# Tile 0's three attention units respaced, and the last tile's weight conversions and load moved later, in a fused attention and two-layer kernel

## The chip, the cores and the metric

The kernel runs on one core of a Trainium2 chip. The metric is the device time of one execution in microseconds (us). The engines are named as the profile names them: PE (TensorE, matrix products), PEld (its weight loads), DVE (VectorE), ACT (ScalarE), POOL (GpSimd) and SP (SyncE, which here only starts DMA transfers; SPq is its queue). Each engine runs its own instructions strictly in order, and waits on the others by semaphores.

## The reference, cut to what matters

```python
# 1. chunked attention, 4 batches x 8 heads x 768 positions x 64: chunks of 32 queries see
#    16 keys to the left, the chunk, 8 to the right, and 8 memory keys
scores = scale * q_c @ k_full.T;  a = softmax(scores);  out_c = a @ v_full
# 2. first layer on 3072 tokens of 512: F1 = 2048
h = x @ w_in;  g = maximum(h, 0) + log1p(exp(-abs(h)));  x1 = g @ w_out
# 3. second layer: F2 = 1536
y = ((x1 @ w_a) * (x1 @ w_b)) @ w_o2
```

## The kernel before, in words

The 3072 tokens are cut into 8 tiles of 384. Every fp32 product is made of three matmuls on split values: a value is rounded to the fp32r type (its high part) and the remainder is kept (its low part), and high x high, high x low and low x high are added up in PSUM.

**Phase 1** runs over tiles t = 0 to 7 and in each over 16 f-steps of 128 of the 2048 hidden columns. An f-step is `emit_h` (12 matmuls into `ph`), `emit_soft` (ACT: abs, exp, ln into `e`; DVE: `g`; then ACT writes the high part `g..h` and DVE or POOL the low part `g..l`), and two steps later (LAG = 2) `emit_x1` (12 matmuls into the four banks `px`). `ph` has two buffers (tag "h"), so `ph` of step f+2 waits until `g` of step f has been read. After step 15 the four `px` are copied out (`xo`, DVE) and stored to DRAM (`x1_scratch`).

**Phase 2** runs over the same 8 tiles: `load_x1` loads a tile back (`xr`) and splits it (`x[:, 0]` a cast on DVE, `x[:, 1]` a subtraction on POOL); 12 steps make `pab` (24 matmuls), the product `c`, and `py`. Three `yo` copies per tile go to the output.

**Weights.** In tile 0 the weights of phase 1 are fetched and converted between the f-steps: a conversion is ACT `raw`, two DVE operations on `tmp`, an ACT cast into `w` and a DVE subtraction into `w` (lines 102 to 113). In tile 7 the weights of phase 2 are fetched and converted the same way, one conversion in an even f-step and two in an odd one.

**Attention.** Tile 0's attention comes ahead of everything, in `Block`s. The tokens of tile t+1 are made during tile t by three `Unit`s of 128 queries: units 3, 4 and 5 in tile 0, units 6, 7, 8 in tile 1, and so on. A unit's steps are: `turn` (DVE transposes k and q into `kt`, `qt`; ACT adds the memory keys to `kt`), `scores` (32 small matmuls into two `sc` banks), `soft` (DVE masks, ACT eight exps into `sm`), `norm_v` (DVE divides), `flip_p` (8 transposes on PE into two `pa` banks, which ACT copies into `af`), `values` (32 matmuls into `pxa`), and `place` (ACT and DVE write the high and low part into the next tile's `x`). `sc`, `pa` and `pxa` share two PSUM buffers (tag "att"), and `kt`, `qt`, `sm` and `af` have one buffer each.

**What sets the order.** A list `plan` holds each step with a due time in slots, two slots to an f-step: slot 2f stands between `emit_soft` of step f and `emit_x1` of step f-2, and slot 2f+1 behind that `emit_x1`. A step is written out at the first slot that isn't below its time. The first three units take their times from `EARLY_STEPS` (offsets) with `place` at `EARLY_AT + EARLY_BY * i` or later. In tile 0 the order on all engines is the written one; in tiles 1 to 7 that holds for PE and DVE alone, and in phase 2 for PE alone; a scheduler places the rest, and it may move instructions of a later stage ahead (the first `raw` of phase 2 stands on ACT in tile 0).

The lines of the plan:

```python
for i, unit in enumerate(units[UPT:]):
    at = 2 * NF1 * (i + 1) // UPT - START
    if i < EARLY:
        at = max(at, EARLY_AT + EARLY_BY * i)
    steps = EARLY_STEPS if i < EARLY else STEPS
    plan += [(at + d - steps[-1][0], i, getattr(unit, step)) for d, step in steps]
```

Of the kernel before, what the change touches and what calls it, by code (L numbers as in the profile page):

```python
# [9 lines left out]
F32 = mybir.dt.float32  # L10
# [3 lines left out]
ALU = mybir.AluOpType  # L14
# [3 lines left out]
TT = 384  # L18
# [3 lines left out]
         (3, "values"), (3.1, "place"))  # L22
START = 1.7
SETS = 1
EARLY_STEPS = ((-7.5, "turn"), (-5.3, "scores"), (-5.2, "soft"), (-3, "norm_v"), (-1.5, "flip_p"),
               (1, "values"), (2, "place"))
EARLY, EARLY_AT, EARLY_BY = 3, 14.5, 8.25

ROUND = ((2, "normal"), (4, "place"), (0, "turn"), (2, "flip"), (1, "scores"), (3, "values"))
EARLY_RAW = (0, 1, 2, 3, 5, 7)  # L30
# [2 lines left out]
CV_ROUND = 1  # L33
CV_AT = (10, 1.5)
LATE = 4
OUT_TAGS = "eegg"


@with_exitstack
def attn_moe_moe2(ctx: ExitStack, tc: tile.TileContext, q, k, v, mem_k, mem_v,  # L40
                  w_in, w_out, w_a, w_b, w_o2, out):
    nc = tc.nc
# [5 lines left out]
    P = 128  # L48
# [17 lines left out]
        name=nc.get_next_instruction_name(), act_func_set_id=6, ins=[], outs=[]))  # L66
# [6 lines left out]
    late = {}  # L73
# [17 lines left out]
    def convert_a(dst, key):  # L91

        u, raw = dst[key]
        words = raw.rearrange("p (n two) -> p two n", two=2)
        low, high = words[:, 0], words[:, 1]
        top = high.bitcast(F32)
        val = mp.tile([P, 512], U32, tag="tmp", name=f"tmp{u}", bufs=2)

        nc.scalar.activation(top, top, AF.Prelu, scale=2.0 ** -112, alpha=-(2.0 ** 32))  # L102

        nc.vector.tensor_scalar(val, low, 29, None, ALU.logical_shift_right)  # L104
        nc.vector.scalar_tensor_tensor(val, high, 3, val, ALU.logical_shift_left, ALU.bitwise_or)  # L105
        dst[key] = u, val.bitcast(F32)
# [25 lines left out]
    def phase2_key(i):  # L132
        f, which = divmod(i, 3)
        return (wab, (which, f)) if which < 2 else (w2o, f)
# [294 lines left out]
# [6 lines that stand above are left out]
# [14 lines left out]
    def split(val, name, engine=nc.gpsimd, between=None):  # L449
        hi = mp.tile([P, TT], F32R, tag="gh", name=name + "h", bufs=3)  # L450
        lo = mp.tile([P, TT], F32R, tag="gl", name=name + "l", bufs=3)
        nc.scalar.copy(hi, val)
        if between:
            between()
        engine.tensor_tensor(lo, val, hi.bitcast(F32), ALU.subtract)
        return hi, lo
# [12 lines left out]
    def emit_soft(t, f, ph, engine=nc.gpsimd, one=None, two=None):  # L469
        e = mp.tile([P, TT], F32, tag="e", name=f"e{t}_{f}")  # L470
        nc.scalar.activation(e, ph, AF.Abs)  # L471
        nc.scalar.activation(e, e, AF.Exp, scale=-1.0)  # L472
        nc.scalar.activation(e, e, AF.Ln, bias=1.0)  # L473
        g = mp.tile([P, TT], F32, tag="g", name=f"g{t}_{f}")
        nc.vector.scalar_tensor_tensor(g, ph, 0.0, e, ALU.max, ALU.add)  # L475
        if one:
            one()
        gt[t, f] = split(g, f"g{t}_{f}", engine, two)

    def emit_x1(t, f):  # L480
# [9 lines left out]
        if f == NF1 - 1:  # L490
            for i in range(KT):
                o = mp.tile([P, TT], F32, tag=OUT_TAGS[i], name=f"xo{t}_{i}")
                nc.vector.tensor_copy(o, acc[t][i][:, :TT])
# [6 lines left out]
    def load_x1(t):  # L500
        raw = late["x"].tile([P, KT, TT], F32, tag="xr", name=f"xr{t}", bufs=1)
        nc.sync.dma_start(raw, x1d[t])
        x = mp.tile([P, 2, KT, TT], F32R, tag="x", name=f"x1_{t}")
        nc.vector.tensor_copy(x[:, 0], raw)  # L504
        nc.gpsimd.tensor_tensor(x[:, 1], raw, x[:, 0].bitcast(F32), ALU.subtract)  # L505
        x1[t] = x

    ct = {}
# [23 lines left out]
    def emit_y(t, f):  # L532
        chh, chl = ct.pop((t, f))
        w = w2o[f]
        if f == 0:
            acc[t] = [ps.tile([P, 512], F32, tag=f"acc{i}", name=f"py{t}_{i}", bufs=1) for i in range(TT // P)]
        for i in range(TT // P):
            s = slice(i * P, (i + 1) * P)
            for m, (a, c) in enumerate(((chh[:, s], w[:, 0]), (chh[:, s], w[:, 1]), (chl[:, s], w[:, 0]))):
                nc.tensor.matmul(acc[t][i], lhsT=a, rhs=c, start=f == 0 and m == 0, stop=f == NF2 - 1 and m == 2)  # L540
        if f == NF2 - 1:
            for i in range(TT // P):
                o = late["x"].tile([P, 512], F32, tag="o", name=f"yo{t}_{i}", bufs=2)
                (nc.vector.tensor_copy if i % 2 else nc.scalar.copy)(o, acc[t][i])
                nc.sync.dma_start(out[t * TT + i * P:t * TT + (i + 1) * P, :], o)
            del acc[t]


    def order():
# [46 lines left out]
        def convert_2(half):  # L596
            n = n_cv2[half]
            if n < (n2, n_cv2[0])[half]:
                if half == 0:
                    convert_a(*phase2_key(n))  # L600
                else:
                    convert_b(*phase2_key(n), late["w"] if n < LATE else None)
                n_cv2[half] += 1

        for t in range(NTILE):
            if t == 1:
                early.close()
                early.enter_context(tc.manual_schedule(engines={engines["P"], engines["V"]}))
            if t == NTILE - 1:
                assert not plan  # L610
                actx.close()
                late["x"] = ctx.enter_context(tc.tile_pool(name="late", bufs=1))
                late["w"] = ctx.enter_context(tc.tile_pool(name="latew", bufs=LATE))
                load_x1(0)
            for f in range(NF1):
                ph = emit_h(t, f)
                if t == 0:
                    due = min(CV_AT[0] + int(CV_AT[1] * (f + 1)), len(uses))
                    fetch_to(due + AHEAD)
                    more = n_cv[0] + 1 < due  # L620
                    convert_1(0)
                    emit_soft(t, f, ph, nc.vector, partial(convert_1, 1), partial(convert_1, 0) if more else None)
                    if more or due == len(uses):
                        convert_1(1)
                elif t < NTILE - 1:
                    emit_soft(t, f, ph)
                else:
                    while n2 < n2_all and n2 < LATE + 2 * max(0, f - LAG):
                        fetch2(n2)
                        n2 += 1  # L630
                    more = f % 2
                    convert_2(0)
                    emit_soft(t, f, ph, nc.vector, partial(convert_2, 1), partial(convert_2, 0) if more else None)
                    if more:
                        convert_2(1)
                att_at(2 * (NF1 * t + f))
                if len(pend) >= LAG:
                    emit_x1(*pend.pop(0))
                pend.append((t, f))
                att_at(2 * (NF1 * t + f) + 1)  # L640
# [55 lines left out]
```

## Time and profile before

| what | us |
|---|---|
| three executions | 1309.62, 1312.18, 1312.55; median 1312.18 |
| the profiled execution, its own time | 1311.32 |
| its span, first to last instruction | 1309.5 |
| PE busy in the span | 1237.2 (94%) |
| DVE busy | 473.4 (36%) |
| ACT busy | 534.7 (41%) |
| POOL busy | 247.6 (19%) |

The span is what the trace shows; 1.8 us of the execution lie outside it. Tile 0's f-steps stand from about 51 to 161 us, tiles 1 to 6 from there to about 611, tile 7 to about 697, and phase 2 from there to the end. In such a profile an engine's idle time counts only where another engine ends up waiting for it, so the table says which engine is nearest to full, and the waits say where time can be won.

### The profile page before, as it was taken

The page shows a single profiled execution, that of the slowest core. Times are in us where ns is not written, and L with a number is a line of the kernel's source. Part 1 is how long each engine was busy: PE and PEld are TensorE (multiplying, and loading weights), DVE is VectorE, ACT ScalarE, POOL GpSimd, SP SyncE. Part 2 cuts the span into 40 slices and gives each one's busy share as a digit, 9 for nine tenths or more (in the row PEclk, how much of TensorE's full clock was granted, in tenths as well). Part 3 has the DMA queues.
Part 4 walks back from the last instruction along what each step waited for, and adds up shares of the span by engine and source line. Part 5 has one row for each costly group of instructions (what it writes and reads, how often), then busy time and mean ns, then how long its engine had stood idle before and what let it go on. Part 6 is the DMA issues. An engine that isn't in the chain of part 4 may idle for free.

```text
span 1309.5 us, 20027 instructions
## 1 busy us (share of the span) xinstructions
PE 1237.2 (94%) x7872; PEld 1170.1 (89%) x7872; DVE 473.4 (36%) x1283; ACT 534.7 (41%) x1328; POOL 247.6 (19%) x233
## 2 busy tenths in 40 slices
PE   5768799999999999999798999999999999999998
PEld 4667699999999999999798999999999999999997
DVE  4767544544444454544678410111101011011100
ACT  4767556555556556554685211111111111111111
POOL 1000023223222322323001011211212121121111
PEclk9879899999999999999899999999999999999999
DMA  8872412213041312211775000010101001000000
GB/s 175 205 246 60 90 37 46 54 35 72 12 73 37 60 48 36 62 23 41 241 227 175 1 26 25 1 49 1 49 1 41 9 10 40 1 25 1 25 1 25
DMA packets 170169, 77.99 MB, mean 60 GB/s; under 512 B 137691, under 2 KB 162395, under 8 KB 170075
## 3 DMA queue, kind: packets, MB, share of 16 engines
q1 hardware_dynamic: 169563, 76.64, 22.1%
q8 instruction: 62, 1.02, 0.3%
q14 instruction: 32, 0.26, 0.1%
q0 software_dynamic: 512, 0.07, 0.0%
HBM read 64.09 MB, written 12.58 MB: 59 GB/s over the span
## 4 chain that ended last, share of the span: by engine, by line
PE 84%; DVE 5%; SPq 3%; ACT 3%; DMA 3%; issue 1%; DVEq 0%; ACTq 0%
PE pab L520 31%; PE ph L465 18%; PE px L488 17%; PE py L540 15%; DMA raw<-in_moe_w_out_dram 2%; PE sc L372 1%; PE pxa L415 1%; SPq L267 1%; DVE w L113 1%; DVE tmp L105 1%; ACT e L472 1%; SPq L264 1%; ACT e L471 1%; ACT e L473 1%; DVE g L475 0%
## 5 line engine op out<-in xcount | busy, mean ns | idle before, releaser
L520 PE MATMUL pab<-x,w 128*128 128x384 f32 x2304 | 418.8, 336 | 4.1 <-issue 4.1
L520 PEld LDWEIGHTS pab<-x,w 128*128 128x128 f32 x2304 | 405.9, 188 | 12.6 <-issue 4.4
L465 PE MATMUL ph<-x,w 128*128 128x384 f32 x1536 | 298.3, 342 | 13.5 <-ACT x L422 8.2
L465 PEld LDWEIGHTS ph<-x,w 128*128 128x128 f32 x1536 | 272.9, 192 | 20.1 <-ACT x L422 9.4
L529 DVE TENSOR_TENSOR c<-pab,a 128x384 f32<-128x384 f32 x96 | 53.6, 558 | 493.5 <-PE pab L520 493.5
L475 DVE SCALAR_TENSOR_TENSOR g<-ph,e 128x384 f32<-128x384 f32 x128 | 71.2, 557 | 257.0 <-ACT e L473 253.3
L527 ACT COPY a<-pab 128x384 f32<-128x384 f32 x96 | 46.1, 480 | 260.4 <-PE pab L520 260.4
L471 ACT ACTIVATE e<-ph 128x384 f32<-128x384 f32 x128 | 62.3, 486 | 132.2 <-PE ph L465 119.5
L390 DVE STREAM_TRANSPOSE af<-sm 32x256 f32<-32x256 f32 x180 | 78.2, 435 | 2.5
L473 ACT ACTIVATE e<-e 128x384 f32<-128x384 f32 x128 | 67.3, 526 | 3.8
L472 ACT ACTIVATE e<-e 128x384 f32<-128x384 f32 x128 | 67.3, 526 | 3.8
L329 ACT ACTIVATE sm<-sm,st 128x96 f32<-128x96 f32 x168 | 60.5, 362 | 4.7 <-DVE st L325 4.7
L505 POOL TENSOR_TENSOR x<-xr,x 128x1536 fp32r<-128x1536 f32 x8 | 28.4, 3554 | 153.5 <-DVE x L504 148.7
L105 DVE SCALAR_TENSOR_TENSOR tmp<-raw,tmp 128x512 uint32<-128x512 uint32 x68 | 50.2, 739 | 14.4 <-ACT raw L102 11.0
L113 DVE TENSOR_TENSOR w<-tmp,w 128x512 fp32r<-128x512 f32 x68 | 46.9, 689 | 16.9 <-ACT w L112 16.8
L102 ACT ACTIVATE raw<-raw 128x512 f32<-128x512 f32 x68 | 45.4, 673 | 15.4 <-DMA raw<-in_moe_w_in_dram 7.1
L112 ACT CAST w<-tmp 128x512 fp32r<-128x512 f32 x68 | 41.6, 613 | 17.2 <-DVE tmp L105 17.1
L195 POOL DMA_DIRECT2D mem_n<-in_mem_k_dram x16 | 8.9, 560 | 155.8 <-DVE mem_t L353 155.8
L336 POOL TENSOR_TENSOR sm<-sm,st 128x768 f32<-128x768 f32 x18 | 26.5, 1472 | 60.1 <-DVE st L334 46.9
L104 DVE TENSOR_SCALAR tmp<-raw 128x512 uint32<-128x512 uint32 x68 | 31.9, 469 | 5.0 <-DMA raw<-in_moe_w_in_dram 4.6
L325 DVE CUSTOM_DVE_ANT_0 sm<-sc,mask 128x96 f32<-128x96 f32 x168 | 31.4, 253 | 3.8 <-PE sc L372 3.8
L329 ACT ACTIVATION_READ_ACCUMULATOR sm<-sm,st 128x1 f32 x168 | 31.4, 187 | 0.0
(251 smaller groups left out, 1851.7 us busy)
## 6 DMA issues: line engine op xcount, KB each, us to landing
raw<-in_moe_w_out_dram SPq DMA_DIRECT2D x28, 512.0 KB
raw<-in_moe_w_in_dram SPq DMA_DIRECT2D x16, 512.0 KB
vn<-in_v_dram SPq DMA_DIRECT2D x35, 176.0 KB
raw<-in_moe_w_a_dram SPq DMA_DIRECT2D x12, 512.0 KB
x_scratch<-xo SPq DMA_DIRECT2D x32, 192.0 KB
xr<-x_scratch SPq DMA_DIRECT2D x8, 768.0 KB
raw<-in_moe_w_b_dram SPq DMA_DIRECT2D x12, 512.0 KB
out_dram<-yo SPq DMA_DIRECT2D x24, 256.0 KB
```

The costliest lines, as they stand in the source:

```text
L105: nc.vector.scalar_tensor_tensor(val, high, 3, val, ALU.logical_shift_left, ALU.bitwise_or)
L113: nc.vector.tensor_tensor(w[:, 1], val, w[:, 0].bitcast(F32), ALU.subtract)
L329: nc.scalar.activation(sm[:, h], sm[:, h], AF.Exp, bias=st[:, 0, h:h + 1], scale=-1.0, accum_out=st[:, 1, h:h + 1])
L390: nc.vector.transpose(out=af[32 * kb:32 * kb + 32, x], in_=self.sm[32 * x:32 * x + 32, :, 32 * kb:32 * kb + 32])
L465: nc.tensor.matmul(ph, lhsT=a, rhs=c, start=n == 0, stop=n == 3 * KT - 1)
L471: nc.scalar.activation(e, ph, AF.Abs)
L472: nc.scalar.activation(e, e, AF.Exp, scale=-1.0)
L473: nc.scalar.activation(e, e, AF.Ln, bias=1.0)
L475: nc.vector.scalar_tensor_tensor(g, ph, 0.0, e, ALU.max, ALU.add)
L488: nc.tensor.matmul(acc[t][i][:, :TT], lhsT=a, rhs=c, start=f == 0 and m == 0, stop=f == NF1 - 1 and m == 2)
L520: nc.tensor.matmul(p, lhsT=a, rhs=c, start=n == 0, stop=n == 3 * KT - 1)
L540: nc.tensor.matmul(acc[t][i], lhsT=a, rhs=c, start=f == 0 and m == 0, stop=f == NF2 - 1 and m == 2)
```

## The change

It does five things. In tile 0 the three units get other offsets: `turn` 13 slots ahead of `place` instead of 9.5, `scores` 10 instead of 7.3, `norm_v` 7 instead of 5, `flip_p` 4 instead of 3.5; and `place` is due at slots 17.4, 24.2 and 31 instead of 14.5, 22.75 and 31, so that a unit's `turn` and `scores` come ahead of the `values` and `place` of the unit in front. In tile 7 the conversions start at step 2 instead of step 0. The first `load_x1` is written at step 7 of tile 7 instead of ahead of it. Its subtraction goes to DVE instead of POOL (for the first tile alone). And `yo` gets three buffers instead of two.

```diff
-EARLY_STEPS = ((-7.5, "turn"), (-5.3, "scores"), (-5.2, "soft"), (-3, "norm_v"), (-1.5, "flip_p"),
-               (1, "values"), (2, "place"))
-EARLY, EARLY_AT, EARLY_BY = 3, 14.5, 8.25
+EARLY_STEPS = ((-13, "turn"), (-10, "scores"), (-9.9, "soft"), (-7, "norm_v"), (-4, "flip_p"),
+               (-1, "values"), (0, "place"))
+EARLY, EARLY_AT, EARLY_BY = 3, 17.4, 6.8
...
+CV2_AT = 2
+X1_AT = 7
...
-        nc.gpsimd.tensor_tensor(x[:, 1], raw, x[:, 0].bitcast(F32), ALU.subtract)
+        (nc.vector if t == 0 else nc.gpsimd).tensor_tensor(x[:, 1], raw, x[:, 0].bitcast(F32), ALU.subtract)
...
-                o = late["x"].tile([P, 512], F32, tag="o", name=f"yo{t}_{i}", bufs=2)
+                o = late["x"].tile([P, 512], F32, tag="o", name=f"yo{t}_{i}", bufs=TT // P)
...
-                load_x1(0)
...
-                    more = f % 2
-                    convert_2(0)
-                    emit_soft(t, f, ph, nc.vector, partial(convert_2, 1), partial(convert_2, 0) if more else None)
+                    if f == X1_AT:
+                        load_x1(0)
+                    more = f >= CV2_AT and f % 2
+                    if f >= CV2_AT:
+                        convert_2(0)
+                    emit_soft(t, f, ph, nc.vector, partial(convert_2, 1) if f >= CV2_AT else None, partial(convert_2, 0) if more else None)
```

What this does to the order of the instructions is seen in three places. In a name such as `ph0_6_950` the first number is the tile and the second the f-step; in `pa0_3_938` the first is the bank and the second the unit; the last is a buffer's number.

PE in tile 0, at the transposes of unit 3 (`flip_p`); before:

```order
L488 MATMUL px0_3_728<-g0_3h_779,w9_641 128x384
L404 MATMUL pa0_3_938<-ident_75,sm3_852 96x128 x4
L404 MATMUL pa1_3_944<-ident_75,sm3_852 96x128 x4
L465 MATMUL ph0_6_950<-x0_395,w10_675 128x384 x12
L488 MATMUL px0_0_725<-g0_4h_830,w11_686 128x384
```

PE at the same transposes, after the change:

```order
L490 MATMUL px0_3_728<-g0_4h_830,w11_686 128x384
L467 MATMUL ph0_7_989<-x0_395,w12_718 128x384 x12
L406 MATMUL pa0_3_1030<-ident_75,sm3_852 96x128 x4
L406 MATMUL pa1_3_1036<-ident_75,sm3_852 96x128 x4
L490 MATMUL px0_0_725<-g0_5h_912,w13_776 128x384
```

The transposes now stand behind `ph` of steps 6 and 7 and `px` of step 4. The scores of unit 4 follow them 12 rows later, behind `px` of step 5.

ACT in tile 0, at the two copies of those transposes into `af`; before:

```order
L112 CAST w17_920<-tmp17_899 128x512
L405 COPY af_83<-pa0_3_938 96x4x128
L405 COPY af_83<-pa1_3_944 96x4x128
L102 ACTIVATE raw19_706<-raw19_706 128x512
L471 ACTIVATE e0_6_969<-ph0_6_950 128x384
```

ACT at the same copies, after the change (`sm4` are the exps of unit 4):

```order
L475 ACTIVATE e0_7_1010<-e0_7_1010 128x384
L114 CAST w19_1016<-tmp19_953 128x512
L454 CAST g0_7h_1019<-g0_7_1014 128x384
L104 ACTIVATE raw21_764<-raw21_764 128x512
L114 CAST w20_1027<-tmp20_1006 128x512
L407 COPY af_83<-pa0_3_1030 96x4x128
L407 COPY af_83<-pa1_3_1036 96x4x128
L331 ACTIVATE sm4_1072,st4_1073<-sm4_1072,st4_1073 128x96 x8
```

The copies now stand behind all of step 7's `e` and `g` work and a conversion, where they stood ahead of step 6's.

DVE at the start of tile 7, from the last `place` on; before (the four `xo` copies of tile 6 follow five rows below the last one shown):

```order
L423 TENSOR_TENSOR x7_6145<-pxa23_6662,x7_6145 128x4x128
L504 CAST x1_0_6691<-xr0_6689 128x1536
L104 TENSOR_SCALAR tmp32_6715<-raw32_6707 128x512
L105 SCALAR_TENSOR_TENSOR tmp32_6715<-raw32_6707,tmp32_6715 128x512
L475 SCALAR_TENSOR_TENSOR g7_0_6723<-ph7_0_6694,e7_0_6719 128x384
L113 TENSOR_TENSOR w32_6725<-tmp32_6715,w32_6725 128x512
L455 TENSOR_TENSOR g7_0l_6729<-g7_0_6723,g7_0h_6728 128x384
L104 TENSOR_SCALAR tmp33_6757<-raw33_6709 128x512
L105 SCALAR_TENSOR_TENSOR tmp33_6757<-raw33_6709,tmp33_6757 128x512
L475 SCALAR_TENSOR_TENSOR g7_1_6765<-ph7_1_6744,e7_1_6761 128x384
```

DVE there, after the change:

```order
L425 TENSOR_TENSOR x7_6145<-pxa23_6662,x7_6145 128x4x128
L477 SCALAR_TENSOR_TENSOR g7_0_6714<-ph7_0_6689,e7_0_6710 128x384
L457 TENSOR_TENSOR g7_0l_6717<-g7_0_6714,g7_0h_6716 128x384
L477 SCALAR_TENSOR_TENSOR g7_1_6749<-ph7_1_6732,e7_1_6745 128x384
L457 TENSOR_TENSOR g7_1l_6752<-g7_1_6749,g7_1h_6751 128x384
L495 COPY xo6_0_6767<-px6_0_6025 128x384
L495 COPY xo6_1_6770<-px6_1_6026 128x384
L495 COPY xo6_2_6773<-px6_2_6027 128x384
L495 COPY xo6_3_6776<-px6_3_6028 128x384
L106 TENSOR_SCALAR tmp32_6792<-raw32_6702 128x512
L107 SCALAR_TENSOR_TENSOR tmp32_6792<-raw32_6702,tmp32_6792 128x512
L477 SCALAR_TENSOR_TENSOR g7_2_6800<-ph7_2_6779,e7_2_6796 128x384
```

The cast of the loaded tile and the three conversions ahead of the `xo` copies have left; the cast and the subtraction stand behind `g7_6l` now.

## Rows read from the trace of the kernel before

**Rows 1.** The page's 40 slices: PE's granted clock in tenths.

```profile
PEclk9879899999999999999899999999999999999999
```

**Rows 2.** By stretch: us, busy PE, PEld, DVE, ACT, POOL, PEclk, DMA, GB/s.

```profile
88.00:93.20 5.20, 5.14 (x19) 5.08 (x20) 0.94 (x2) 1.73 (x3) 0.00 (x0) 0.50 0.27 88
107.00:111.00 4.00, 4.00 (x16) 4.00 (x15) 3.43 (x20) 3.09 (x14) 0.00 (x0) 0.57 0.01 2
702.60:1302.60 600.00, 600.00 (x3163) 562.66 (x3163) 92.62 (x164) 112.43 (x224) 106.60 (x90) 1.00 0.06 21
```

**Rows 3.** PE's waits, 66 to 170 us: total us, times, longest.

```profile
PE pa L404 <- DVE sm L336: 17.4, 3, 11.0
```

**Rows 4.** Timeline, tile 0: start, us, engine, operation [idle before <- releaser].

```profile
88.06 1.91 PE L404 MATMUL pa<-ident,sm 128*96 128x128 f32 x8 [11.02 <-DVE sm L336]
...
105.66 0.88 PE L372 MATMUL sc<-kt,qt 64*64 64x96 f32 x28 [0.51 <-DVE x L423]
...
119.17 1.05 PE L404 MATMUL pa<-ident,sm 128*96 128x128 f32 x8 [2.50 <-DVE sm L336]
...
160.98 0.44 PE L465 MATMUL ph<-x,w 128*128 128x384 f32 x1 [4.10 <-ACT x L422]
...
86.95 0.96 DVE L336 TENSOR_TENSOR sm<-sm,st 128x768 f32<-128x768 f32 x1
...
121.08 1.06 ACT L405 COPY af<-pa 96x512 f32<-96x512 f32 x2
```

**Rows 5.** PE's waits, 606 to 700 us.

```profile
PE px L488 <- DVE xo L493: 6.9, 1, 6.9
PE pab L520 <- issue: 4.1, 1, 4.1
```

**Rows 6.** The chain that ended last, tile 7: start, us, what.

```profile
616.01 0.96 DVE x L504
617.34 3.88 DVE tmp L105
621.24 3.83 DMA raw<-in_moe_w_out_dram
630.98 4.18 PE px L488 x12
637.77 2.08 PE px L488 x12
665.34 2.39 PE ph L465 x12
674.48 2.37 PE ph L465 x12
```

**Rows 7.** Timeline, first matmuls of tile 7, and its end.

```profile
612.92 2.20 PE L465 MATMUL ph<-x,w 128*128 128x384 f32 x11 [0.28 <-DVE x L423]
...
691.26 3.77 POOL L505 TENSOR_TENSOR x<-xr,x 128x1536 fp32r<-128x1536 f32 x1 [70.60 <-DVE x L504]
691.64 3.67 DVE L104 TENSOR_SCALAR tmp<-raw 128x512 uint32<-128x512 uint32 x1
```

**Rows 8.** The end: last matmuls (timeline) and last copy (chain).

```profile
1303.18 0.62 PE L540 MATMUL py<-w,c_11h 128*128 128x512 f32 x2
...
1305.44 0.58 ACT yo L544
```

**Rows 9.** The chain, tile 0.

```profile
78.04 2.98 ACT sm L329 x16
81.01 0.54 ACT raw L102
83.06 0.56 DVE g L475
```

**Rows 10.** Timeline of SP: first and last key and query loads of tile 2.

```profile
130.59 0.33 SPq L185 DMA_DIRECT2D kn<-in_k_dram  x1
...
150.72 0.47 SPq L187 DMA_DIRECT2D qn<-in_q_dram  x1
```

## The prediction

> **What bounds the kernel now.** First the busy times by stretch: from 702.6 us on PE is busy in 600.00 of 600.00 us at the full clock [rows 2], so phase 2 can only be moved as a whole. Then the slices of PE's clock, which fall below 9 at the front and in the slice of 622 to 655 us [rows 1]: these are tile 0 and the start of tile 7, and there PE stands idle. Then PE's waits in these two stretches. In tile 0 the transposes of the normalised scores wait three times, 17.4 us in all, 11.0 the first time [rows 3], and the first step of tile 1 waits 4.10 us for the last `place` [rows 4]. In tile 7 one wait of 6.9 us is for the `xo` copies, and one of 4.1 stands ahead of phase 2 [rows 5]. The reader should see that PE waits here for DVE and ACT, whose work per step is about as long as PE's.
>
> What an idle PE also costs is its clock: behind the wait of 11.02 us it ran at 0.50, the lower of its two levels (1.2 GHz), from 88.0 to 93.2, which loses 2.6 us of full-rate work [rows 2, 4].
>
> **The change in tile 0.** No operation is added or removed; I lay out the new order with the durations of the trace.
>
> *Up to 87.9 us nothing moves but PE.* ACT's and DVE's orders are the same through the normalisation of unit 3, which ends at 86.95 + 0.96 = 87.91 [rows 4]. In the 11.02 us that PE idled it now does `ph` of step 6 and `px` of step 4 (2.08 us each, the length of twelve such matmuls at the full clock [rows 6]), and `ph` of step 7 as soon as `g` of step 5 has been read at 83.06 + 0.56 [rows 9]. The transposes start at about 87.95 as before, with 6.2 us more of PE's work done.
>
> *The next wait.* The scores of unit 4 now follow one `px` behind those transposes, and take over their two PSUM banks: they wait for ACT's two copies, which have moved behind step 7's activations. From 87.9 on DVE does a pair of `tmp` operations, `g`, `w`, `g..l` of step 6 and the two `kt` transposes (3.7 us by the starts in this stretch of the timeline), so ACT adds the memory keys until 91.9; from `raw` to the end of `g` is 81.01 to 83.62, 2.6 us [rows 9], which gives 94.6 for step 7; the cast of `g`, a `raw` and a `w` cast (1.55) and the two copies (1.06 [rows 4]) give 97.2. PE has only 3.1 us of work meanwhile, so it idles for some 6 us, and I take a half-rate stretch of 5.2 us behind it. The scores start at 97.2 where they started near 105.66 [rows 4].
>
> *Once more.* At half rate the scores end at 98.9 and `ph` of step 8 at 102.8; the exps (2.98 [rows 9]) and a `raw` end at about the same time. Steps 8 and 9 follow at 2.6 us from activation to `g`, PE's `ph` between them; the normalisation of unit 4 ends at 114.6, its transposes on PE at 115.7, and the copies, behind the whole chain of step 10, at 120.7. PE idles 5.0 us, another half-rate stretch; the scores of unit 5, at 132 before, start at 120.7. In the same way `ph` of step 11 ends at 126.3, the exps of unit 5 at 134.7, the transposes of unit 5 at 141.0, `g` of step 14 at 147.3 and of step 15 at 150.5. Behind it DVE still transposes for unit 6 ahead of the last `place`, so tile 1 starts at 153.7 instead of 160.98 [rows 4]: **7.3 us**. A wait of about 3.2 us is left there.
>
> Bounds: without the two half-rate stretches (2.6 to 2.9 each) the same layout ends near 148, 13 us earlier than before. With one more such stretch on the path and half a microsecond of slip, 4 us remain. The layout is nearest to what the trace shows behind long waits, so I take 7.3.
>
> *Queues.* The loads of keys and queries for tile 2 need 20.6 us of SP (130.59 to 151.19 [rows 10]) from the transposes of unit 5 on, then come the values of unit 5. They now start near 117 and end near 138; the values are used near 147. So they stay hidden, by about 5 us with their landing; if that cover went, each microsecond over it would be one at tile 1's start. Two weight loads now stand ahead of the values of unit 4 on SP; they wait for buffers freed near 93, and are hidden.
>
> **The change in tile 7.** Removed ahead of the `xo` copies: the cast (0.96), the `tmp` operation held for 3.88 beside POOL's subtraction, and three conversions, the last of which waited for a load of 3.83 [rows 6]. DVE then has `g`, `g..l` of steps 0 and 1 and the copies, done from 623.4 on; PE, which does five groups of 2.08 from 612.9 on [rows 7], can start `px` of step 0 near 623.5 instead of 630.98, and at the full clock (2.08 instead of 4.18). `px` of step 1, at 637.77 before [rows 6], would start at 627.6: 10.2 us.
>
> Given back: (1) The fourth weight load now waits for the buffer of `w_in`'s step 2, free at 623.5; it lands 3.83 later at 627.4, and ACT has its `raw` and a `w` cast ahead of step 2's activations, so `g` of step 2 ends at 631.2, and `ph` of step 4 waits 1.5 us for it. Below: nothing, if the load were early; above: 4, if it lands as late as others that share the engines. I take 1.5. (2) From step 8 on two steps take 674.48 - 665.34 = 9.14 us [rows 6] instead of four groups of 2.08, 8.32, because ACT and DVE pass a conversion back and forth. Now that starts at step 4, two pairs earlier: 1.6 us. (3) The cast and the subtraction at step 7 load DVE. The subtraction on DVE isn't in the trace: 384 elements take 0.56 [rows 9] and 768 take 0.96 [rows 4], so 1536 take 0.96 + 2 x 0.40 = 1.8 us, below POOL's 3.77 [rows 7]. Of the 2.7 us together, none (DVE waits for ACT in each pair) to all can fall on PE; I take 1.5. Together **5.6 us** of 10.2 remain; bounds 1.5 and 9.
>
> Not changed: the second `load_x1` keeps POOL's subtraction, which holds DVE for 3.67 [rows 7], so the wait of 4.1 us ahead of phase 2 stays. Three conversions move into phase 2 (about 5.4 us of DVE); PE is covered there, since DVE is busy in 92.62 of 600 us [rows 2], and would lose at most that 5.4.
>
> **The third buffer.** The last copy waited for a store to free its buffer, and started at 1305.44; the last matmul ended at 1303.18 + 0.62 [rows 8]. It can start at 1303.85, 1.6 us earlier; three stores then overlap, so I take **1.4**, bounds 0.8 and 1.6. In the other tiles such waits lie beside a full PE.
>
> **Sum.** 7.3 + 5.6 + 1.4 = 14.3 us off the profiled execution's own 1311.32 gives 1297.0. That execution is 0.9 below the median of the runs; I forecast 1297.5.
>
> **Rivals.**
> - *PE keeps its clock in tile 0.* The transposes behind 2.50 us of idle took 1.05, the full rate [rows 4]. If the copies come sooner than I laid out, the waits are short like that one: 13 + 5.6 + 1.4, so 1291. Against it: ACT's order puts whole steps ahead of the copies.
> - *The last tile gives little.* Loads land late, step 2 starts late and DVE never catches up: 1.5 us there, so 1301.
> - *The waits in tile 0 only move*, from the transposes to the scores, and the last `place` comes when it came: 1304. Against it, 6.2 us of PE's work are certainly moved into idle time; but PE isn't what ACT and DVE wait for most.
> - *PE stays at half rate through the rest of tile 0*, the one that ends slower. The stretch from 107 to 111 ran at 0.57 [rows 2] though the waits just ahead, the last of 0.51 [rows 4], were short; the new order has six waits of 1.6 to 6 us. From 81.2 on PE has 45.5 us of work in tile 0, 91 at half rate: tile 1 would start at 172, 11 later than before, less 7 elsewhere: 1316. It decides from about 20 us of further half-rate time on. Against it, full rate came back within 5.2 us each time. The Trainium skill, "TensorE: Matmul & The Clock Gate", section "What's actually happening", says that the throttled clock is the default and activity releases it; by that rule taken strictly each new wait would cost rate, and the sum would come out at this rival's time; the row at 119.17 speaks against it, that of 107 to 111 for it.
>
> **Chances.** Forecast 0.60; clock kept 0.15; last tile gives little 0.17; waits only move 0.05; half rate throughout 0.03. The range leaves out the half-rate case and the far ends: 1289 (both terms near their upper bounds) to 1304.5 (the moved waits, or both near the lower ones). What a measurement of this kernel can tell from no change is about 0.2%, 2.6 us. Faster by more: 0.94; within: 0.03; slower: 0.03.
>
> **What would show it.** Right: PE's wait for `pa` of unit 3 short, and waits of 5 to 6 us ahead of the scores of units 4 and 5 ended by ACT's copies, with a half-rate stretch behind each; tile 1 starting near 153.7; in tile 7 no wait for `xo`, and 9.1 us a pair from step 4 on; the 4.1 us ahead of phase 2 still there; the last copy at the last matmul. Wrong: no half-rate stretch in tile 0, a wait on a load of values or of `raw`, or DVE stalled at step 7's cast.

## The result, and the profile after

The changed kernel takes 1295.44 us (median of 4 runs, 1294.76 to 1295.87) against 1312.26 (4 runs, 1309.62 to 1312.55) for the kernel before: ratio 0.9872, 95% interval 0.9856 to 0.9888. That is 16.8 us less; forecast were 14.3 off, 1297.5. Its profiled execution took 1295.8 with a span of 1294.0.

First PE's waits from 66 to 166 us (total us, times, longest); they answer to [rows 3].

```profile
PE sc L374 <- ACT af L407: 9.9, 2, 5.6
PE ph L467 <- DVE g L477: 2.5, 1, 2.5
PE ph L467 <- ACT x L424: 2.0, 1, 2.0
PE pxa L417 <- issue: 1.9, 1, 1.9
PE pa L406 <- DVE sm L338: 0.9, 2, 0.5
```

The transposes `pa`, which had waited 17.4 us, wait 0.9; instead the two sets of scores `sc` wait for ACT's copies, as forecast (5 and 6 us). The timeline of tile 0, answering to [rows 4]:

```profile
82.31 3.87 PE L467 MATMUL ph<-x,w 128*128 128x384 f32 x12 [2.46 <-DVE g L477]
...
86.69 1.05 PE L406 MATMUL pa<-ident,sm 128*96 128x128 f32 x8 [0.51 <-DVE sm L338]
...
95.40 2.02 PE L374 MATMUL sc<-kt,qt 64*64 64x96 f32 x32 [5.58 <-ACT af L407]
...
118.46 2.03 PE L374 MATMUL sc<-kt,qt 64*64 64x96 f32 x32 [4.34 <-ACT af L407]
120.42 3.86 PE L467 MATMUL ph<-x,w 128*128 128x384 f32 x12
...
130.29 1.80 PE L417 MATMUL pxa<-af,vn 96*64 96x64 f32 x32 [1.86 <-issue]
...
151.96 0.44 PE L467 MATMUL ph<-x,w 128*128 128x384 f32 x1 [2.05 <-ACT x L424]
152.69 2.21 PE L467 MATMUL ph<-x,w 128*128 128x384 f32 x11 [0.28 <-DVE x L425]
```

Scores of 2.02 and a `ph` of 3.87 are work at the lower clock (0.89 and 2.24 at the full one). By stretches the granted clock there reads (columns as in [rows 2]):

```profile
93.00:98.00 5.00, 2.60 (x34) 2.19 (x35) 3.90 (x15) 3.22 (x9) 0.00 (x0) 0.50 0.27 98
118.00:123.00 5.00, 4.54 (x40) 4.13 (x41) 1.54 (x4) 1.47 (x3) 0.00 (x0) 0.50 0.49 117
130.00:134.00 4.00, 3.71 (x38) 3.62 (x39) 1.94 (x14) 3.97 (x19) 0.00 (x0) 0.57 0.42 67
```

Tile 1 starts at 151.96 instead of 160.98 [rows 4], 9.02 us earlier. 1.36 of that is no work of the change: the normalisation of unit 3 already ended 1.36 earlier, and the first `ph` of tile 0 started between 48.5 and 51.5 us in the profiles of this study, old and new layout alike. 7.66 remain. Another 1.5 follow, because tile 1 now begins at the full clock (2.21 for eleven matmuls; 3.75 at 161.70 before).

In tile 7 PE's waits, then the timeline (answering to [rows 5] and [rows 6, 7]), and one row of the chain of waits:

```profile
PE ph L467 <- DVE g L477: 4.3, 6, 1.5
PE pab L522 <- issue: 4.1, 1, 4.1
PE px L490 <- DVE g_9l L457: 0.8, 1, 0.8
```

```profile
620.70 2.37 PE L467 MATMUL ph<-x,w 128*128 128x384 f32 x12 [1.42 <-DVE g L477]
...
649.48 2.37 PE L467 MATMUL ph<-x,w 128*128 128x384 f32 x12 [0.26 <-DVE g L477]
...
668.56 2.37 PE L467 MATMUL ph<-x,w 128*128 128x384 f32 x12 [0.26 <-DVE g L477]
...
681.57 6.88 PE L522 MATMUL pab<-x,w 128*128 128x384 f32 x24 [4.14 <-issue]
...
641.25 1.76 DVE L507 TENSOR_TENSOR x<-xr,x 128x1536 fp32r<-128x1536 f32 x1
...
676.60 3.67 DVE L106 TENSOR_SCALAR tmp<-raw 128x512 uint32<-128x512 uint32 x1
```

```profile
644.42 8.64 DMA raw<-in_moe_w_b_dram
```

The wait of 6.9 us for `xo` is gone, the 4.1 us ahead of phase 2 have stayed. The three `ph` rows are steps 4, 10 and 14, by counting the groups from the first at 602.38. Last the end, answering to [rows 8]:

```profile
1289.51 0.39 PE L542 MATMUL py<-w,c_11l 128*128 128x512 f32 x1
1289.93 0.59 ACT L546 COPY yo<-py 128x512 f32<-128x512 f32 x1 [0.77 <-PE py L542]
```

The last copy now waits for the last matmul and for nothing else.

So the 15.5 us between the two spans (1309.5 and 1294.0) split into 1.36 at the front, 7.66 in tile 0, 1.5 at the start of tile 1, 4.5 in tile 7 (the lead grows from 612.92 - 602.38 = 10.54 to 696.61 - 681.57 = 15.04), 0.9 given back by the first group of phase 2 (6.88 instead of 5.97), and 1.4 at the end.

### The profile page after: what moved, and what is told of

Read it like the earlier page. It is cut to its first block, busy times and chain, and to the rows that moved or that the text cites. A ratio compares the mean times of both kernels' runs of the same rounds, so it can differ in the third digit from the quotient of the medians.

```text
span 1294.0 us, 20030 instructions
## 1 busy us (share of the span) xinstructions
PE 1236.5 (96%) x7872; PEld 1168.0 (90%) x7872; DVE 471.4 (36%) x1284; ACT 535.6 (41%) x1328; POOL 244.4 (19%) x232
## 4 chain that ended last, share of the span: by engine, by line
PE 84%; DVE 4%; SPq 4%; ACT 3%; DMA 3%; issue 1%; DVEq 0%
PE pab L522 31%; PE ph L467 18%; PE px L490 16%; PE py L542 15%; DMA raw<-in_moe_w_out_dram 2%; PE sc L374 1%; PE pxa L417 1%; SPq L269 1%; DMA raw<-in_moe_w_b_dram 1%; DVE w L115 1%; DVE tmp L107 1%; SPq L266 1%; ACT e L474 1%; SPq L189 1%; ACT raw L104 1%
## 5 line engine op out<-in xcount | busy, mean ns | idle before, releaser
L507 POOL TENSOR_TENSOR x<-xr,x 128x1536 fp32r<-128x1536 f32 x7 | 25.0, 3572 | 153.5 <-DVE x L506 79.0
L107 DVE SCALAR_TENSOR_TENSOR tmp<-raw,tmp 128x512 uint32<-128x512 uint32 x68 | 47.0, 692 | 11.2 <-ACT raw L104 7.3
L114 ACT CAST w<-tmp 128x512 fp32r<-128x512 f32 x68 | 41.5, 614 | 15.1 <-DVE tmp L107 14.9
```

## The experiments

Each was timed beside the kernel before, in four sets; the changed kernel was in none of them. So where a run is set against the changed kernel or against another run, the two times can come from different sets, in which the kernel before has medians from 1310.57 to 1312.99. The first three take the change apart.

**Tile 0 alone.**

```diff
-EARLY, EARLY_AT, EARLY_BY = 3, 14.5, 8.25
+EARLY, EARLY_AT, EARLY_BY = 3, 17.4, 6.8
...
```

(with the new `EARLY_STEPS`, on the kernel before)

> Only the new order of tile 0's steps; conversions of the last tile and the two output buffers as before. If the terms add: tile 1's first matmul moves from 160.98 to about 152 to 153.3 (7.7 us out of the waits; 1.4 more would be the front of the kernel that happened to run earlier), another 1.5 us since tile 1 no longer begins with a half-rate stretch, so 9 us in all, near 1303, ratio .993. If the gain of the whole change in tile 0 needs the other parts (or its size was an accident of that profile): less than 5 us, over 1307.

Measured: 1302.19 against 1311.38, ratio 0.993 (0.9917 to 0.9943), 9.2 us. In its profile tile 1 starts at 153.18, 7.8 us earlier than before (1.0 of it from the front), and at the full clock (2.21 for eleven matmuls). The terms add: first theory.

**The last tile alone.**

```diff
-EARLY, EARLY_AT, EARLY_BY = 3, 17.4, 6.8
+EARLY, EARLY_AT, EARLY_BY = 3, 14.5, 8.25
...
-                o = late["x"].tile([P, 512], F32, tag="o", name=f"yo{t}_{i}", bufs=TT // P)
+                o = late["x"].tile([P, 512], F32, tag="o", name=f"yo{t}_{i}", bufs=2)
```

(on the changed kernel, with the old `EARLY_STEPS`)

> Only the last tile's part: conversions from step 2 on, the first load of the second phase's rows at step 7 with its subtraction on VectorE; tile 0's steps and the two output buffers as before. By the trace of the whole change: 4.5 us less in tile 7 and 0.9 given back at the start of phase 2, so 3.6 us, near 1308.5, ratio .997. By the prediction's own term: 5.6 us, 1306.5. If the delayed loads cost more when tile 7 starts later: under 2 us, not to be told from no change.

Measured: 1306.39 against 1311.38, ratio 0.9964 (0.9951 to 0.9976), 5.0 us: between the two sizes that were named, and the interval holds both.

**The third buffer alone.**

```diff
-                o = late["x"].tile([P, 512], F32, tag="o", name=f"yo{t}_{i}", bufs=2)
+                o = late["x"].tile([P, 512], F32, tag="o", name=f"yo{t}_{i}", bufs=TT // P)
```

> Only the third output buffer. If the last copy waited for a store to free its buffer: the last copy starts with the end of the last matmul, the tail shrinks from 5.7 to about 4.3 us, 1.4 us in all (1310.8, ratio .999), which these rounds can just about tell. If three stores that overlap hold one another up: the copy starts early and the end moves by under 0.5 us.

Measured: 1310.41 against 1311.38, ratio 0.9992 (0.9982 to 1.0002): 1.0 us by the medians, not told apart from nothing by time. The trace shows the step itself: the last copy starts 0.43 behind the start of the last matmul, as in the changed kernel (0.42). The three medians add up to 15.2 of the 16.8 us.

**An idle PE kept busy.** In the changed kernel, matmuls that nobody reads stand ahead of the scores of units 4 and 5.

```diff
+WARM = {4: 24, 5: 18}
...
+            if u in WARM:
+                d = ps.tile([P, 512], F32, tag="h", name=f"warm{u}")[:, :TT]
+                for _ in range(WARM[u]):
+                    nc.tensor.matmul(d, lhsT=w1[0][:, 0, 0:P], rhs=xt[0][:, 0, 0, :], start=True, stop=True)
```

> The whole change, and in tile 0 added matmuls whose result nobody reads, about 5 us of them ahead of the scores of unit 4 and 4 us ahead of those of unit 5, where TensorE otherwise stands idle for 5.6 and 4.3 us; nothing is left out. Theory, that each idle stretch costs a half-rate stretch which lies on the path: the granted clock behind the two sets of scores is 1.0, ph of steps 8 and 11 takes 2.1 instead of 3.5 and 3.9 us, tile 1 starts 2 to 5 us earlier and the run comes to 1291 to 1293.5. Rival, that ScalarE and VectorE set the pace there: the clock rises all the same, but the waits ahead of later work grow by what it gave; under 1 us in all, 1294.5 to 1296. If the added matmuls reach past the wait: slower, 1297 or more.

Measured: 1293.12 (1292.08 to 1293.48), ratio 0.9858 (0.9842 to 0.9875). The runs lie 2.3 us below those of the changed kernel and don't overlap with them, the intervals of the ratios do. The timeline:

```profile
88.49 4.32 PE L371 MATMUL warm<-x,w 128*128 128x384 f32 x24
94.26 1.35 PE L379 MATMUL sc<-kt,qt 64*64 64x96 f32 x32 [1.44 <-ACT af L412]
...
146.46 4.62 PE L472 MATMUL ph<-x,w 128*128 128x384 f32 x12 [2.88 <-ACT x L429]
```

From 94 to 100 and from 116 to 121 the granted clock is 1.00. Tile 1 starts 5.5 us earlier than in the changed kernel, 0.8 of it from the front and 4.7 from tile 0 itself. Of that, 2.3 are lost again by the start of tile 7 (452.0 us from the one to the other here, 449.7 in the changed kernel), since tile 1's own first `ph` now falls to the lower clock. The theory holds, with 2.3 us at the low end of its range: the half-rate stretches behind the scores went, and one came at the start of tile 1.

**The first subtraction back on GpSimd.**

```diff
-        (nc.vector if t == 0 else nc.gpsimd).tensor_tensor(x[:, 1], raw, x[:, 0].bitcast(F32), ALU.subtract)
+        nc.gpsimd.tensor_tensor(x[:, 1], raw, x[:, 0].bitcast(F32), ALU.subtract)
```

> The whole change, but the first subtraction of the second phase's rows (step 7 of the last tile) goes back to GpSimd. Theory, that a VectorE operation beside it is held for its length: one tmp operation takes 3.7 to 3.9 us instead of about 0.5, VectorE is free 1.5 to 2 us later than with the subtraction of 1.76 on itself, and step 8's wait of 1.5 us becomes 3 to 3.5: 1297 to 1297.5. Rival, that GpSimd's subtraction lies beside the waits that the pairs have anyway: within 0.5 us of the whole change.

Measured: 1298.82 (1295.89 to 1300.64), ratio 0.9899 (0.9884 to 0.9915), 3.4 us slower than the changed kernel, more than was expected (the intervals of the ratios just overlap). The timeline at step 7:

```profile
644.10 3.52 POOL L507 TENSOR_TENSOR x<-xr,x 128x1536 fp32r<-128x1536 f32 x1 [39.50 <-DVE x L506]
...
648.69 3.81 PE L467 MATMUL ph<-x,w 128*128 128x384 f32 x12 [2.86 <-DVE g L477]
```

and of VectorE:

```profile
644.33 3.84 DVE L107 SCALAR_TENSOR_TENSOR tmp<-raw,tmp 128x512 uint32<-128x512 uint32 x1
...
649.92 0.69 DVE L107 SCALAR_TENSOR_TENSOR tmp<-raw,tmp 128x512 uint32<-128x512 uint32 x1
```

The same operation takes 0.69 by itself and 3.84 beside POOL. The next `ph` waits 2.86 instead of 1.51 and runs at the lower clock, 3.81. Tile 7 takes 81.84 us (first `ph` to first `pab`) instead of 79.92, which is the 1.9 that was expected. This execution also began tile 1, far ahead of the edit, at the lower clock (4.10 for its first twelve matmuls), worth 1.2 (450.9 us from the start of tile 1 to that of tile 7, 449.7 in the changed kernel); whether that is the rest in the other runs too, their times alone don't tell.

**Conversions from step 0 again, the rows still at step 7.**

```diff
-CV2_AT = 2
+CV2_AT = 0
```

> The whole change, but the last tile's conversions start at step 0 again; the first rows of the second phase still come at step 7. Theory, that the conversions ahead of the xo copies hold them: three conversions and a wait for a load come back there, without the cast (0.96) and the held operation (3.88): px of step 0 waits some 3 to 5 us and runs at half rate; of tile 7's 4.5 us one to 3 are lost: 1297 to 1298.5. Rival, that the load of the second phase's rows with its held operation was all of the wait of 6.9 us: the time stays at 1295, or falls, since the saturated pairs start with less work left.

Measured: 1300.54, ratio 0.9918 (0.9905 to 0.9932): 5.1 us slower than the changed kernel, more than either theory gave. Tile 7 takes 84.13 us, which leaves 0.3 of the 4.5. A row of the timeline and one of the chain of waits:

```profile
618.58 0.66 PE L490 MATMUL px<-g_0h,w 128*128 128x384 f32 x1 [4.59 <-DVE xo L495]
```

```profile
611.57 4.49 DMA raw<-in_moe_w_b_dram
```

The wait for `xo` is back at 4.59, behind a conversion that waits for its load. So of the 6.9 us [rows 5] the conversions made about two thirds; moving the rows alone gains next to nothing, since they cost at step 7 what they free at step 0: against the kernel before, tile 7 is 2.9 us ahead at its step 8, 1.0 at step 10 and 0.3 at its end.

**The second subtraction on VectorE too.**

```diff
-        (nc.vector if t == 0 else nc.gpsimd).tensor_tensor(x[:, 1], raw, x[:, 0].bitcast(F32), ALU.subtract)
+        (nc.vector if t <= 1 else nc.gpsimd).tensor_tensor(x[:, 1], raw, x[:, 0].bitcast(F32), ALU.subtract)
```

> The whole change, and the second subtraction of the second phase's rows (at the start of phase 2) on VectorE too. Theory, that GpSimd's subtraction holds VectorE for 3.67 us and so makes the wait of 4.1 us ahead of phase 2: the held operation shrinks to about 0.5, with 1.76 for the subtraction in its place, the wait falls to 2 to 2.5 us, and the first group of phase 2 (6.88 us at half rate) gets nearer to its 4.1 at the full clock: 2 to 4 us, 1291.5 to 1293.5. Rival, that the wait is for a weight load or for ScalarE: it stays within 0.5 us of 4.1, and the time at 1295.

Measured: 1292.73 (1292.40 to 1293.03), ratio 0.9856 (0.9841 to 0.9871), 2.7 us faster than the changed kernel by the medians, 2.1 by the ratios, whose intervals overlap.

```profile
676.33 0.42 DVE L106 TENSOR_SCALAR tmp<-raw 128x512 uint32<-128x512 uint32 x1
...
676.67 1.75 DVE L507 TENSOR_TENSOR x<-xr,x 128x1536 fp32r<-128x1536 f32 x1
...
678.94 0.55 DVE L477 SCALAR_TENSOR_TENSOR g<-ph,e 128x384 f32<-128x384 f32 x1
...
679.59 5.97 PE L522 MATMUL pab<-x,w 128*128 128x384 f32 x24 [2.43 <-issue]
```

The `tmp` operation falls from 3.67 to 0.42, the wait ahead of phase 2 from 4.14 to 2.43, and the first group from 6.88 to 5.97: 2.6 us together. Theory right. The group takes over the bank of `ph` of step 14 and starts 0.10 us behind the end of `g` of that step (678.94 + 0.55), as it does in the changed kernel (681.47, then 681.57); so what the trace put down to "issue" is VectorE, held by GpSimd there and busy with the subtraction here.

**Transposes and copies a step earlier in tile 0.**

```diff
-EARLY_STEPS = ((-13, "turn"), (-10, "scores"), (-9.9, "soft"), (-7, "norm_v"), (-4, "flip_p"),
+EARLY_STEPS = ((-13, "turn"), (-10, "scores"), (-9.9, "soft"), (-7, "norm_v"), (-5.3, "flip_p"),
```

> The whole change, but in tile 0 the transposes of the normalised scores and ScalarE's copies of them come a step earlier, ahead of the next step's activations on ScalarE. Theory, that the waits of 5.6 and 4.3 us ahead of the scores of units 4 and 5 come from the copies standing behind that step: these waits fall under 2.5 us, with no half-rate stretch behind them, and tile 1 starts up to 4 us earlier: 1291 to 1294. Rival, that the wait only moves back to the transposes, which stand on TensorE ahead of ph of the next step and wait for the normalisation (the first wait of the kernel before, 11 us): waits for sm of 4 to 8 us, and 1296 to 1300.

Measured: 1292.94 (1290.83 to 1294.85), ratio 0.9858 (0.9841 to 0.9874), 2.5 us faster by the medians, 1.8 by the ratios, whose intervals overlap.

```profile
86.60 1.91 PE L406 MATMUL pa<-ident,sm 128*96 128x128 f32 x8 [6.83 <-DVE sm L338]
...
93.42 0.89 PE L374 MATMUL sc<-kt,qt 64*64 64x96 f32 x32
...
110.52 1.91 PE L406 MATMUL pa<-ident,sm 128*96 128x128 f32 x8 [6.40 <-DVE sm L338]
...
117.34 0.89 PE L374 MATMUL sc<-kt,qt 64*64 64x96 f32 x32
...
149.03 0.45 PE L467 MATMUL ph<-x,w 128*128 128x384 f32 x1 [2.05 <-ACT x L424]
```

Each theory was half right. The waits of the scores are gone, but they moved back to the transposes, longer than before (6.8 and 6.4) and with the lower clock behind them (1.91). Yet tile 1 starts 2.9 us earlier in this profile; 1.1 of it stands at the scores of unit 5 already (117.34, not 118.46), the rest comes behind them. My reading is that the way from one unit's scores through exps, normalisation, transposes and copies to the next unit's scores counts, and not how long PE stands still on it. One profile doesn't show that: the next run's, with the same order in tile 0, starts tile 1 later, though by the medians the edit is worth 1.9 there too (1290.79 against 1292.73).

**Both edits**, of the last two runs:

> The whole change with the two edits that helped by themselves: the transposes and copies in tile 0 a step earlier (2.5 us by its median) and the second subtraction of the second phase's rows on VectorE (2.7). If they add, being in tile 0 and at the end of tile 7: tile 1 starts near 149, phase 2 starts after a wait of 2.4 us, and the run comes to about 1290.2. If the earlier start of tile 7 meets loads that are not there yet: more than 1291.5.

Measured: 1290.79 (1290.58 to 1292.91), ratio 0.984 (0.9826 to 0.9853). By the medians they add, within 0.6 us. The profile is that of the slowest execution (1292.91), and tile 1 doesn't start near 149 in it:

```profile
151.84 0.44 PE L467 MATMUL ph<-x,w 128*128 128x384 f32 x1 [2.05 <-ACT x L424]
```

The half-rate stretches behind the transposes last longer here: the `ph` behind them take 4.19 and 4.04, where the eighth run has 3.24 and 3.25. The wait ahead of phase 2 is 2.42, as expected.

**Both edits, and PE kept busy in tile 0.** The unread matmuls stand ahead of the transposes.

```diff
+WARM = {3: 36, 4: 32}
...
+                for _ in range(WARM.get(self.u, 0) * (j == 0)):
+                    nc.tensor.matmul(bank[:, :TT], lhsT=w1[0][:, 0, 0:P], rhs=xt[0][:, 0, 0, :], start=True, stop=True)
```

> The kernel with both edits, and in tile 0 added matmuls that nobody reads, 6.2 and 5.5 us of them, written into the bank of the transposes ahead of those of units 3 and 4, where TensorE stands idle for 6.8 and 6.4 us; nothing is left out. Theory, that an idle TensorE loses its clock and the slower work behind it lies on the path from the transposes to the next scores: the transposes and ph of the next step run at 1.0 instead of 0.5, that is 0.8 and 1.7 us each time, tile 1 starts 2 to 5 us earlier, 1285.5 to 1288.5. Rival, that what follows waits for ScalarE and VectorE anyway: within 1 us of the kernel with both edits.

Measured: 1289.34 (1286.68 to 1291.37), ratio 0.9822 (0.9808 to 0.9835): 1.4 us below the run without, intervals overlapping, so between the two theories and not settled by time.

```profile
86.43 1.05 PE L410 MATMUL pa<-ident,sm 128*96 128x128 f32 x8 [0.62 <-DVE sm L339]
...
147.77 0.44 PE L471 MATMUL ph<-x,w 128*128 128x384 f32 x1 [2.47 <-ACT x L428]
```

The clock is full behind the transposes. Tile 1 starts 4.1 us earlier than in the profile of the run without the fill (151.84), but only 1.3 us earlier than at 149.03 in the eighth run, which has the same order in tile 0. Whether the clock or the order of ScalarE's and VectorE's work sets more of it stays open. This is the fastest median of the study, some 22 us below the kernel before.

**The clock alone, in the kernel before.** The same fill ahead of the transposes of unit 3.

```diff
+WARM = {3: 36}
...
```

> The kernel before, with 6.2 us of unread matmuls ahead of the transposes of unit 3, in its wait of 11.0 us; nothing is left out. It tells how much of the gain in tile 0 could have come from the clock alone. If the half-rate stretch behind that wait lies on the path: from 88 on the granted clock is 1.0, and 1.5 to 2.6 us are gained, ratio .998 to .9988. If the layout decides (the order of the steps, with ScalarE and VectorE setting the pace): the clock is full and the time within 1 us of before.

Measured: 1311.52 against 1311.68, ratio 0.9994 (0.9986 to 1.0003): nothing. But the trace says something else than the second theory:

```profile
86.61 1.05 PE L408 MATMUL pa<-ident,sm 128*96 128x128 f32 x8 [2.92 <-DVE sm L337]
...
101.72 0.96 PE L373 MATMUL sc<-kt,qt 64*64 64x96 f32 x28 [0.51 <-DVE x L427]
...
159.90 4.36 PE L469 MATMUL ph<-x,w 128*128 128x384 f32 x12 [6.52 <-ACT x L426]
```

The clock came back, and the scores of unit 4 came 2.5 us earlier after these transposes (15.1 behind them, 17.6 in the kernel before [rows 4]); that lead is lost by the start of tile 1. The timeline of ScalarE at the end of tile 0, first in the kernel before and then in this run:

```profile
155.06 0.66 ACT L102 ACTIVATE raw<-raw 128x512 f32<-128x512 f32 x1 [6.11 <-DMA raw<-in_moe_w_a_dram]
```

```profile
153.98 0.65 ACT L103 ACTIVATE raw<-raw 128x512 f32<-128x512 f32 x1 [7.31 <-DMA raw<-in_moe_w_a_dram]
```

This is the first weight of phase 2, which is not used for some 540 us. Its load stands on SP behind the loads of keys and queries (it went out at 151.30, the last of those at 150.72 [rows 10]), and the conversion that waits for it stands on ACT ahead of step 15's activations. The last run tests that.

**The load ahead of the last eight key and query loads**, with the fill of the run above:

```diff
+            if unit.u // UPT == 1:
+                plan[-1] = (28.2, i, plan[-1][2])
+                plan.append((28.1, i, partial(fetch2, 0)))
...
-        n2 = 0
+        n2 = 1
```

> The kernel before with the added unread matmuls of the last run, and the weight load that ScalarE waited for at the end of tile 0 (6.1 us before, 7.3 with the added matmuls) ahead of the last eight loads of keys and queries on SP instead of behind them. Theory, that this load held the end of tile 0 in the kernel before and took back what the clock gave: its wait falls under 1 us, ScalarE starts step 15 about 4.5 us earlier, the last place waits for the transposes of unit 6 alone, tile 1 starts 3 to 4.5 us earlier than with the added matmuls alone, and the ratio to the kernel before is .996 to .9975. Rival, that another wait stands right behind it (the loads of keys and queries that are now later, or the values of unit 5): under 1 us, .9985 or more.

Measured: 1307.52 against 1312.99, ratio 0.9957 (0.9943 to 0.9972), clear of the run above.

```profile
150.22 0.67 ACT L103 ACTIVATE raw<-raw 128x512 f32<-128x512 f32 x1 [2.49 <-DMA raw<-in_moe_w_a_dram]
...
156.52 0.45 PE L472 MATMUL ph<-x,w 128*128 128x384 f32 x1 [2.05 <-ACT x L426]
```

ScalarE still waits 2.49, not under 1, but it is ready at 150.9, about when the `ph` it needs is; tile 1 starts 3.4 us earlier, and from the end of unit 5's normalisation to tile 1 it takes 12.41 us instead of 16.86. Theory right; the gain over the run above is 4.8 us by the two ratios and 2.5 between the two profiled executions. Tile 1 came earlier with the lower clock behind the transposes of unit 3 (1.83 in this execution, the fill notwithstanding), so this gain is the load's.

## Why the prediction came out

**Tile 0** (7.3 forecast, 7.66 read, 9.2 with tile 1's start when run alone). The layout holds step by step: shifted by the front's 1.36, the scores of unit 4 came at 96.8 (97.2 forecast), those of unit 5 at 119.8 (120.7), the transposes of unit 5 at 140.6 (141.0), the end of `g` of step 15 at 150.1 (150.5), tile 1 at 153.3 (153.7). The waits of 6 and 5 us for ACT's copies were there (5.58 and 4.34), with a half-rate stretch behind each; two more stretches, behind 2.46 us ahead of step 7's `ph` and 1.86 ahead of `pxa`, were not laid out. That the gain came within 0.4 us is in part luck: from the end of unit 3's normalisation to tile 1 the three profiles of the old order take 73.1 to 73.8 us and the five of the new one 65.3 to 66.9, so single profiles could have given anything from 6.2 to 8.5.

What the layout did not see is on the other side of the subtraction. The 160.98 from which it was taken was itself late: a weight load held ScalarE for 6.11 us, and step 15's activations started at 155.62, 2.1 us after their `ph` had ended (151.01 + 2.50). I had read the loads of keys and queries as hidden, and asked only what they cover for the values; the load queued behind them on the same queue was the one that ended the tile. In the new order ScalarE does that conversion behind step 15's activations, at 148.09 and without a wait. So about 2 of the 7.66 us come from a wait that the change removed by the way. The last run, which differs from the one before it in the load alone, shows that it held the tile's end; no run moves it without the unread matmuls, and that just 2 us of the whole change are its share is worked out, not run.

The half-rate stretches were priced at 2.6 to 2.9 each. Filling two idle waits in the changed kernel took 1.8 us out between the scores of units 4 and 5, where one stretch went (21.27 us instead of 23.06), and 2.6 from there to tile 1, where two did (30.93 instead of 33.50): on the path a stretch cost less than its price. The time fell by 2.3 alone, since a new stretch at the start of tile 1 took half of it back. In the faster kernel the fill gave 1.4, not settled, and in the kernel before nothing, since the load held the tile's end.

The 1.5 us at the start of tile 1 were not in the sum. Against its 14.3 the two profiled executions differ by 15.5: 0.4 more in tile 0, 1.4 at the front and 1.5 at tile 1's start, less 1.1 in tile 7 and 0.9 in phase 2. By the medians it is 16.8; where the other 1.3 lie the profiles don't show.

**Tile 7** (5.6 forecast, 4.5 read, 5.0 when run alone). The gross gain was sized right: by step 4 the tile is ahead by 8.45 us of its own (639.69 - 612.92 before, 620.70 - 602.38 after), and 1.42 more but for the wait forecast at 1.5, so 9.9 where 10.2 were laid out. From step 4 to step 10, 3.13 are given back; the two terms for it, saturated pairs and the subtraction, were 1.6 and 1.5. (The 9.14 that I read is the pair from step 10 on; that from step 8 on took 9.01. After the change the pairs from step 4 on take 9.2, 8.7, 10.8, 9.9 and 9.1, not 9.1 throughout.) The subtraction took 1.76 on VectorE, 1.8 estimated. The step that failed is a missing one: the load of 8.64 us ahead of step 12, which costs 0.82 between steps 10 and 14. I had priced only the first of the loads that the later start delays. SP shows where this one stood:

```profile
632.92 0.37 SPq L89 DMA_DIRECT2D raw<-in_moe_w_b_dram  x1
643.04 0.34 SPq L504 DMA_DIRECT2D xr<-x_scratch  x1
```

The rows of phase 2 have one buffer (`xr`). The first of them still went out ahead of tile 7, at 601.11; what moved to step 7 is their cast and subtraction, so the second load of rows waited on SP for 10.0 us, until that subtraction was done (641.25 + 1.76), with the weight loads behind it in the queue. Then four loads went out within 1.4 us, the one of 8.64 last. That they would have cost nothing without the hold is not tested.

**Phase 2.** The 4.1 us stayed, as forecast, and the seventh run shows the cause that was read from two overlapping rows [rows 7]. That the first group behind an equal wait would take 6.88 instead of 5.97 was not foreseen; in the profiles of this study it took 5.82 to 7.17 behind 4.1 us, and 4.40 to 6.00 behind 2.4.

**The third buffer** (1.4): 1.4 by the trace, 1.0 by the medians. The size is luck. I had taken the end of the wrong matmul; one more follows the row that I read [rows 8]:

```profile
1303.63 0.39 PE L540 MATMUL py<-w,c_11l 128*128 128x512 f32 x1
```

It ends at 1304.02, so only 1.4 of the 1.6 were there to win, and the discount of 0.2 for overlapping stores made up for it.

**The rivals.** *PE keeps its clock* is what the fourth run brought about in part of tile 0, and that was worth 4.7 us in tile 0 but 2.3 of time, not 5.7. *The last tile gives little* fell with 4.5 to 5.0 us. *The waits only move* is true of PE's waits and wrong of the time, twice over: the eighth run moved them once more and gained again. *Half rate throughout* did not come: full rate was back after 4 to 6 us each time.

## What to carry to other kernels

Where PE waits in turn for ScalarE and VectorE, lay out the way from one unit to the next through all three engines, and don't count PE's idle time: it moved twice here while the kernel got faster. Before taking a stage's end as the place to subtract from, ask what ended it; a prefetch nobody needs yet, in an in-order queue behind small loads and with its consumer ahead of urgent work, can be the answer. And an operation that went to an idle engine to spare a busy one should be timed together with what it holds up: GpSimd's 3.5 us held VectorE for 3.2 (3.84 instead of 0.69), VectorE alone needed 1.76.

## What was unexpected of the hardware

The clock behind a wait can't be read from the wait. The first `ph` of tile 1 waits 2.05 us in the changed kernel and in seven of the runs. Behind that it ran at the full clock in five of the eight profiles (2.18 to 2.21 for eleven matmuls), at the lower one in one (4.10 for twelve), and changed over within the group in two (2.90 and 3.30 for eleven). In the same way the transposes of unit 3 took 1.05 behind an idle 2.92 in one run and 1.83 behind 2.88 in the next, with the same fill ahead. The Trainium skill, "TensorE: Matmul & The Clock Gate", section "What's actually happening", says that the number of matmuls at the slow clock, counted from a kernel's start, varies between runs of one kernel; these rows show the same for waits in the middle of one. The spread of tile 0 goes with it: in five profiles of the same layout it took 102.0 and 102.1 us (first `ph` of tile 0 to first of tile 1) where the two `ph` behind the scores took 3.4 to 3.9 us, and 103.6 to 104.1 where they took 4.0 to 4.2. That the one makes the other is likely, not shown.

That VectorE is held for nearly the whole of a GpSimd operation was known from [rows 7]; the fifth run adds that an operation on two inputs is held in the same way (3.84 instead of 0.69). The Trainium skill, "SBUF — State Buffer", section "SBUF: two separate sides", says that where the two contend, the one that starts first gets the ports they share for the whole instruction and the other is blocked; the trace agrees (GpSimd started at 644.10, the held operation at 644.33).
